# Gated attention plus token-mixing MLP: the last 24 attention visits in eight groups of three instead of twelve groups of two

## The chip, the cores and the metric

The kernel runs on one core of a Trainium2 chip. The metric is the device time of one execution in microseconds (us). Every time below comes from the runs of the kernel before or from the profile of one of its executions.

## The reference

The input x has S = 2048 tokens of D = 640 channels, in float32. Two branches read it and a gate mixes them:

```python
g = sigmoid((x * gate_w).sum(-1))
# attention: 32 heads of 20, one shared K and V
q = x @ wq; k = x @ wk; v = x @ wv
p = softmax(q k^T * 20**-0.5)          # per head, 2048 x 2048
a = concat_heads(p @ v) @ wo
# token mixing MLP
h = layernorm(x)
u = gelu(h^T @ w1 + b1)                # over tokens, F = 1728
b = (u @ w2 + b2)^T
out = g * a + (1 - g) * b
```

## The kernel before

**Units and visits.** Attention is cut into 32 units: four blocks of 512 queries times eight groups of four heads. For each unit the 2048 keys are walked in 16 blocks of 128, so there are 512 (unit, key block) pairs, which the code calls `units` and which I call visits. A visit needs four score tiles, one per head: `qk(u, pr, b)` issues one matmul of 62 rows by 512 columns on TensorE (L632) into a PSUM tile `s`, and one exponential on ScalarE (L635) from `s` into an SBUF tile `p`. The pool `ps_s` has three PSUM buffers, so the fourth score has to wait until the first exponential has read its tile, and so on; the pool `pp_pool` has twelve `p` buffers. `pv_mm(u)` then issues the four products with V (L659), which use four column tiles of 32 and accumulate over the unit's 16 visits in the one PSUM tile `o` (`ps_o`, one buffer). After a unit's last visit VectorE transposes `o` out of PSUM (L668), and the next unit's first product has to wait for that.

**Lanes.** A score needs 62 rows of the array only. Scores with b = 0 use rows 0 to 63 and those with b = 1 rows 64 to 127, and the other matmuls of the loop are cut into halves of 64 rows as well. The kernel writes out by hand (`manual_schedule`) an order in which the two row halves, the lanes, each have a list of work, and it interleaves the two lists by adding up estimated times: `X_US` = 0.232 us for a score, `F_US` = 0.147 us for a matmul with 320 columns. Each engine works through its instructions in the order in which they are written.

**The main loop.** For visits 0 to 487 each step k writes four scores in lane k % 2 (two of visit k - 1 and two of visit k) and other work in the other lane, then the four products of visit k - 1. Each head pair of a visit belongs to one lane, so half the scores of a visit are written one step early.

**The last 24 visits.** When the other work has run out (`TAIL` = 24, `k_tail` = 488), the lanes are filled with the output projection of the last eight blocks of 128 tokens. `tail_job(n)` (L773) puts its matmuls on the two lists `tail[0]` and `tail[1]`, 216 and 204 of them; `tail_take` takes the next ones from a list. They accumulate in the pools `ps_m` (three PSUM buffers) and `ps_g` (one), and each finished tile is scaled and added by VectorE (L780), which frees its buffer. `tail_load` fetches their operands by DMA (L754, L757). `stretch(k, n)` writes the scores of the steps k to k + n - 1 and their share of the tail matmuls, interleaved, and then the products of the visits k - 1 to k + n - 2, together. It is called once with n = 1 (the single) and then twelve times with n = 2 (the doubles). Where in a lane's list its scores stand is given by fixed fractions (`cut`) of its tail matmuls.

**Behind it.** After the last products come 24 matmuls of held partial sums (L1012), the chain that scales and splits the last unit's output (L668 to L685), 24 last matmuls (L1026) and the stores. `settle` pops pieces of the chain of an earlier unit, `visit` writes the products and, at two key blocks of a unit, the store and the fetch of the row maxima (L491, L498) that the next unit's scores need. These go on SyncE's DMA queue, as do the stores of finished output rows (L784).

Of the kernel before, what the change touches and what calls it, by code (L numbers as in the profile page):

```python
# [9 lines left out]
F32 = mybir.dt.float32  # L10
# [7 lines left out]
P = 128  # L18
# [6 lines left out]
NB = 512  # L25
# [12 lines left out]
def mix_kernel(ctx: ExitStack, tc: tile.TileContext, A_x, A_wq, A_wk, A_wv, A_wo,  # L38
               B_x, B_w1, B_b1, B_w2, B_b2, gate_w, out):
    nc = tc.nc  # L40
    x = A_x[0]
    y_out = out[0]

    def f32(ap):
        return ap.bitcast(F32)
# [30 lines left out]
    right = ExitStack()  # L76
# [73 lines left out]
    def new_q(n):  # L150
        if n < NU:
            qtiles[n] = load_q(n, "qst")
# [13 lines left out]
    with tc.tile_pool(name="pa", bufs=1) as pa, \  # L166
# [129 lines left out]
        def q_parts(m, ts):  # L296
            cols = slice(m * P, (m + 1) * P)
            return [[(wq_hi[:, c, cols], ts[c][0]) for c in range(DC)],
                    [(wq_hi[:, c, cols], ts[c][1]) for c in range(DC)],
                    [(wq_lo[:, c, cols], ts[c][0]) for c in (0, 3, 1, 4, 2)]]  # L300
# [88 lines left out]
        for sb in range(NQB):  # L389
# [11 lines left out]
            for m in range(DC):  # L401
# [3 lines left out]
                p = q_parts(m, ts)  # L405
# [36 lines left out]
    pp_pool = ctx.enter_context(tc.tile_pool(name="pp", bufs=12))  # L442
# [112 lines left out]
    with tc.tile_pool(name="psb", bufs=2, space=PSUM, side="right") as psb:  # L555
        at, skip, last = 0, 3, NS * PRO - 6
# [40 lines left out]
    oTs = [slot[1][:, 2 * DC * D + i * 2 * D:2 * DC * D + (i + 1) * 2 * D].rearrange("p (j c q) -> p j c q", j=2, q=P)  # L597
           for i in range(2)]
    yts = [f32(slot[1][:, 2 * DC * D + 4 * D + i * D:2 * DC * D + 4 * D + (i + 1) * D]) for i in range(2)]
    pools = {}  # L600

    def second():
        right.close()
        pools["rows"] = ctx.enter_context(tc.tile_pool(name="rows", bufs=3, side="right"))

    wos = {}
# [10 lines left out]
    units = [(n, kb) for n in range(NU) for kb in range(NS)]  # L617
# [4 lines left out]
    SYNC = mybir.DependencyInfo(mybir.DependencyClass.Sync, mybir.DependencyReason.DATA)  # L622
    odd_s = [0]

    def qk(u, pr, b):
        n, kb = units[u]
        if kb == 4 and pr == 0 and b == 0:
            new_q(n + 1)
        q = qtiles[n]
        odd_s[0] ^= 1  # L630
        s = ps_m.tile([P, NB], F32, name="ms") if spare[0] and odd_s[0] and not loaded else ps_s.tile([P, NB], F32, name="s")
        nc.tensor.matmul(s, kst[64 * b:64 * b + 62, kb * P:(kb + 1) * P], q[64 * b:64 * b + 62, pr, :],  # L632
                         start=True, stop=True)
        p = pp_pool.tile([P, NB], F32, name="p")
        nc.scalar.activation(p, s, AF.Exp, scale=SCALE)  # L635
        ptiles[u, 2 * pr + b] = p

# [97 lines left out]
    tail = [[], []]  # L735
    loaded = []
    CUT = 3 * P
    HEAD = (H - 4) * DH
    jobs = [(st, 0, D) for st in range(NS - 8, NS - 4)]
# [7 lines left out]
    def tail_load(i):  # L747
        if i < len(jobs):
            st, r0, r1 = jobs[i]
            cols = slice(st * P, (st + 1) * P)  # L750
            oT, yt = room(i)
            c0, c1 = r0 // P, r1 // P
            for j in range(2):
                nc.sync.dma_start(out=f32(oT[:, j, c0:c1]),  # L754
                                  in_=o_scr[j, r0:c1 * P, cols].rearrange("(c p) s -> p c s", p=P))
                if r1 > c1 * P:
                    nc.sync.dma_start(out=f32(oT[:r1 - c1 * P, j, c1]), in_=o_scr[j, c1 * P:r1, cols])  # L757
            if r0 == 0:
                nc.sync.dma_start(out=yt, in_=y_scr[cols, :])
            loaded.append(i)  # L760
# [31 lines left out]
    def tail_take(h, n):  # L792
        out = []
        while len(out) < n and tail[h] and tail[h][0][0] in loaded:
            out.append(tail[h].pop(0)[1])
        return out
# [56 lines left out]
    def b1_jobs(d, fc):  # L853
        hold = {}
        base = 4 * (d * FC + fc)

        def load():
            pass

        def mm(st, k, half):  # L860
            if not hold.get("n"):
                hold["p"], hold["n"] = ps_g.tile([P, NB], F32, name="g"), 0
            wh, wl = w1t[base + st // HS]
            w, h = ((wh, h_hi), (wh, h_lo), (wl, h_hi))[k]
            hold["n"] += 1
            r = slice(64 * half, 64 * half + 64)
            other_tile(half, nc.tensor.matmul(hold["p"][:, :HD2], w[r, st % HS, :], h[d][r, st, :],  # L867
                                              start=(hold["n"] == 1), stop=(hold["n"] == 6 * NS)))

        def done():  # L870
            gelu(d, fc, [hold["p"]])

        return load, [([[lambda h=h, st=st, k=k: mm(st, k, h) for h in range(2)]
                        for st in range(NS) for k in range(3)], done)]

    def batches(tiles, counts):
        out = []
        for n, (load, parts, *_) in enumerate(tiles):
            for d, (steps, done) in enumerate(parts):
                cnt = counts.pop(0)  # L880
                rows = [[f[h] for f in steps if len(f) > h] for h in range(2)]
                cut = [[len(r) * j // cnt for j in range(cnt + 1)] for r in rows]
                for j in range(cnt):
                    rest = []
                    if d == 0 and j == 0 and n + 1 < len(tiles):
                        rest.append(tiles[n + 1][0])
                    out.append(([r[c[j]:c[j + 1]] for r, c in zip(rows, cut)], rest, [done] if j == cnt - 1 else []))
        return out

    k_tail = len(units) - TAIL  # L890
    todo = [divmod(i, FC) for i in range(PRO, 2 * FC)]
    seq = batches([b1_jobs(*t) for t in todo], [5] * len(todo))
    for i, (steps, rest, done) in enumerate(seq):
        item, j = divmod(i + 1, 5)
# [17 lines left out]
    for i, k in enumerate((443, 451, 459, 467, 473, 477, 481, 485)):  # L912
        ph[k][1].append(lambda i=i: tail_load(i))

    X_US, F_US = 0.232, 0.147

    def beside(rows0, rows64, x):
        lanes = [list(rows0), list(rows64)]
        at = [0.0, 0.0]
        while lanes[0] or lanes[1]:  # L920
            k = 0 if lanes[0] and (not lanes[1] or at[0] <= at[1]) else 1
            if k == x and len(lanes[k]) == 1 and lanes[1 - k]:
                k = 1 - k
            us, f = lanes[k].pop(0)
            f()
            at[k] += us
# [15 lines left out]
    def settle(k):  # L942
        for _ in range(2 if spare[0] else 1):
            f = later.pop(0) if later else None
            if f:
                f()
        pop_chain()

    def visit(u):
        pv_mm(u)  # L950
        n, kb = units[u]
        if kb == 7 and n + 1 < NU:
            store_max(n + 1)
        if kb == 9 and n + 1 < NU:
            fetch_max(n + 1)

    for k in range(k_tail):
        b = k % 2
        ss = [lambda u=u, pr=pr: qk(u, pr, b) for u in (k - 1, k) for pr in range(2) if u >= 0]
        fs, rest, done = ph[k]  # L960
        ms = [[f for f in (ms_next(x) for _ in range(c)) if f] for x, c in (((b, 3), (1 - b, 1)) if len(fs) < 12 else ((b, 4), (1 - b, 0)))]
        lanes = [None, None]
        lanes[b] = lane_x(ss, ms[0])
        lanes[1 - b] = lane_f(ms[1], fs, done)
        if k == 0:
            (m0, m1, m2), (s0, s1) = ms[0], ss
            lanes[0] = [(3 * X_US, m0), (3 * X_US, m1), (X_US, s0), (X_US, m2), (X_US, s1)]
        beside(*lanes, b)
        ms_done()
        spare[0] = len(row_max) == NU  # L970
        settle(k)
        for f in rest:
            f()
        if k == k_tail - 4:
            raw = last_wo()
        if k == k_tail - 2:
            w_last = split_last(raw)
        if k:
            visit(k - 1)

    def stretch(k, n):
        lanes = [None, None]
        for b in range(2):
            own = [j for j in range(k, k + n) if j % 2 == b]
            ss = [lambda u=u, pr=pr, b=b: qk(u, pr, b) for j in own for u in (j - 1, j) for pr in range(2) if u < len(units)]
            fs = tail_take(b, math.ceil(len(tail[b]) * n / (len(units) + 1 - k)) + (n == 1) * (3 if not ss else -3))
            cut = [0] + [round(len(fs) * x) for x in ((0.25, 0.5, 0.75, 1.0) if n == 1 else
                                                          (0.18, 0.53, 0.82, 1.0) if b == k % 2 else (0.41, 0.71, 1.0, 1.0))]
            lanes[b] = [x for i in range(4) for x in [(X_US, y) for y in ss[i:i + 1]] +
                        [(F_US, f) for f in fs[cut[i]:cut[i + 1]]]]  # L990
        beside(*lanes, None)
        for j in range(k, k + n):
            settle(j)
            if 13 <= j - k_tail < 17:
                tail_load(8 + j - k_tail - 13)
            visit(j - 1)

    stretch(k_tail, 1)
    for k in range(k_tail + 1, len(units), 2):
        stretch(k, 2)  # L1000
    accs = {}

    for c in range(CUT // P, DC):
# [14 lines left out]
    for i in range(4):  # L1018
        st = NS - 4 + i
        for d in range(2):  # L1020
            at = pp_pool.tile([P, NB], F32, name="p")
# [34 lines left out]
```

## Time and profile before

| | |
|---|---|
| median of 3 runs (lowest to highest) | 1699.42 us (1699.42 to 1699.83) |
| the profiled execution's own time | 1699.95 us |
| its span, first to last instruction | 1698.2 us |
| visits 488 to 511, doubles only | 1617.84 to 1685.55 us of the span |
| behind the last products | 1685.55 to 1698.2 us |

How to read it: times are counted from the start of the span. A row of the timeline gives the start, the time from the start of the first to the end of the last of the instructions merged in the row, the engine, the line, the operation with its tiles, and the number of instructions. PE is TensorE (matmuls), PEld its weight loads, DVE VectorE, ACT ScalarE, POOL GpSimd, SPq the DMA issues of SyncE. Two row halves of the array work at once, so rows of PE overlap. A product with V stands as two instructions in the profile, hence x16 for two visits.

### The profile page before, as it was taken

Reading aid. Unit: us, or ns where it says so; the run is one execution under the profiler, and the core shown is the slowest. Engines: PE = TensorE matmul, PEld = TensorE weight load, DVE = VectorE, ACT = ScalarE, POOL = GpSimd, SP = SyncE. Lnnn points to the kernel's source line nnn. Section 1 sums busy time; section 2 is a strip of 40 time slices with the busy share of each in tenths; the row PEclk is TensorE's granted clock in tenths of the full one; section 3 lists DMA queues with packets and bytes.
Section 4 is the critical chain, followed back from the end, with each engine's and each line's share of the span. In section 5 each row is a group of like instructions: output and inputs, shape, how many; then the busy total and the mean of one; then the engine's idle time right before and its main releaser. Section 6 shows DMA issues by size and latency. Waiting matters only on the chain.

```text
span 1698.2 us, 39056 instructions
## 1 busy us (share of the span) xinstructions
PE 1690.9 (100%) x14865; PEld 1102.9 (65%) x14865; DVE 1434.7 (84%) x2915; ACT 1190.0 (70%) x2322; POOL 570.8 (34%) x723
## 2 busy tenths in 40 slices
PE   9999999999999999999999999999999999999998
PEld 7899766666666666666666666666666666555666
DVE  6679898888888888888888888888888888888734
ACT  4445677777777777777777777777777777777775
POOL 6467644544445454322222222222221111111200
PEclk9999999999999999999999999999999999999999
DMA  7665322222222222121212222222111222334411
GB/s 208 196 182 143 93 64 69 65 61 67 59 69 70 70 70 70 48 64 53 58 47 70 71 59 62 63 56 62 51 51 38 58 63 64 95 109 146 133 54 57
DMA packets 173377, 135.45 MB, mean 80 GB/s; under 512 B 32729, under 2 KB 139382, under 8 KB 173190
## 3 DMA queue, kind: packets, MB, share of 16 engines
q1 hardware_dynamic: 173190, 132.96, 28.0%
q8 instruction: 117, 1.92, 0.5%
q14 instruction: 70, 0.57, 0.1%
HBM read 100.27 MB, written 31.65 MB: 78 GB/s over the span
## 4 chain that ended last, share of the span: by engine, by line
PE 97%; issue 2%; DVE 1%; POOL 0%; ACT 0%; POOLq 0%; DVEq 0%; ACTq 0%
PE o L659 30%; PE s L632 18%; PE ms L466 17%; PE g L704 12%; PE g L867 8%; PE pp L293 4%; PE pu L576 4%; PE g L816 2%; PE ms L773 1%; PE pt L285 0%; PE pp L357 0%; DVE mp L469 0%; PE g L773 0%; PE pp L182 0%; PE pp L285 0%
## 5 line engine op out<-in xcount | busy, mean ns | idle before, releaser
L469 DVE TENSOR_REDUCE mp<-ms 128x1 f32<-128x512 f32 x2048 | 1278.6, 684 | 171.3 <-PE ms L466 167.2
L635 ACT ACTIVATE p<-s 128x512 f32<-128x512 f32 x2048 | 1069.1, 604 | 397.5 <-PE s L632 394.0
L466 PE MATMUL ms<-kst,qmx 60*128 60x512 f32 x2048 | 847.5, 421 | 0.7 <-DVE mp L469 0.5
L632 PE MATMUL s<-qst,kst 62*128 62x512 f32 x2048 | 745.6, 404 | 0.0
L659 PE MATMUL o<-p,v_sb 128*32 128x512 f32 x4096 | 554.6, 604 | 0.0
L466 PEld LDWEIGHTS ms<-kst,qmx 60*128 60x128 f32 x2048 | 378.0, 185 | 213.4 <-DVE flag L645 176.9
L632 PEld LDWEIGHTS s<-qst,kst 62*128 62x128 f32 x2048 | 378.0, 186 | 11.5 <-issue 10.9
L867 PE MATMUL g<-slot,wh 64*128 64x320 f32 x1152 | 281.6, 318 | 0.0
L124 POOL TENSOR_TENSOR wl<-wr,wh 128x512 fp32r<-128x512 f32 (+1 forms) x176 | 220.6, 1255 | 34.7 <-ACT wh L121 20.9
L867 PEld LDWEIGHTS g<-slot,wh 64*128 64x128 f32 x1152 | 190.6, 184 | 59.9 <-DVE flag L645 59.9
L123 POOL CAST wh<-wr 128x512 fp32r<-128x512 f32 (+1 forms) x136 | 79.7, 586 | 444.2 <-PE g L704 281.3
L704 PE MATMUL g<-slot,wh 64*128 64x320 f32 x864 | 209.0, 317 | 0.0
L704 PE MATMUL g<-u,wh 64*128 64x320 f32 x864 | 208.8, 317 | 0.0
L659 PEld LDWEIGHTS o<-p,v_sb 128*32 128x32 f32 x4096 | 93.3, 108 | 138.1 <-issue 130.8
L867 PE MATMUL g<-slot,wl 64*128 64x320 f32 x576 | 179.4, 311 | 0.0
L704 PEld LDWEIGHTS g<-slot,wh 64*128 64x128 f32 x864 | 142.3, 184 | 40.3 <-DVE flag L645 40.3
L704 PEld LDWEIGHTS g<-u,wh 64*128 64x128 f32 x864 | 142.3, 184 | 40.3 <-DVE flag L645 40.3
L704 PE MATMUL g<-u,wl 64*128 64x320 f32 x432 | 134.9, 313 | 0.0
L704 PE MATMUL g<-slot,wl 64*128 64x320 f32 x432 | 134.9, 313 | 0.0
L867 PEld LDWEIGHTS g<-slot,wl 64*128 64x128 f32 x576 | 106.0, 184 | 15.1 <-DVE flag L645 15.1
L704 PEld LDWEIGHTS g<-u,wl 64*128 64x128 f32 x432 | 79.5, 184 | 13.4 <-DVE flag L645 13.4
L704 PEld LDWEIGHTS g<-slot,wl 64*128 64x128 f32 x432 | 79.4, 184 | 13.4 <-DVE flag L645 13.4
(195 smaller groups left out, 1405.2 us busy)
## 6 DMA issues: line engine op xcount, KB each, us to landing
wr<-in_B_w_dram SPq DMA_DIRECT2D x152, 256.0 KB
qmx<-q_scr SPq DMA_DIRECT2D x192, 80.0 KB
qst<-q_scr SPq DMA_DIRECT2D x192, 80.0 KB
y_scr<-yo SPq DMA_DIRECT2D x16, 320.0 KB
slot<-o_scr SPq DMA_DIRECT2D x16, 320.0 KB
o_scr<-oh SPq DMA_DIRECT2D x124, 40.0 KB
o_scr<-ol SPq DMA_DIRECT2D x124, 40.0 KB
q_scr<-qh SPq DMA_DIRECT2D x19, 256.0 KB
```

What stands on the lines that cost most here:

```text
L123: nc.gpsimd.tensor_copy(wh, wr)
L124: nc.gpsimd.tensor_sub(wl, wr, f32(wh))
L293: nc.tensor.matmul(pp, w, t, start=first and n == 0, stop=not more and n == len(steps) - 1)
L466: nc.tensor.matmul(ms, qmax[n][64 * b:64 * b + 60, pr, qt * P:(qt + 1) * P], kst[64 * b:64 * b + 60, kq * NB:(kq + 1) * NB], start=True, s ...
L469: nc.vector.tensor_reduce(mtiles[n][:, c, kq:kq + 1], ms, axis=AX.X, op=ALU.max)
L576: nc.tensor.matmul(pu[r][:, :HD2], w[rows, c, :], h[rows, st, :], start=(st == 0 and k == 0), stop=(st == NS - 1 and k == 2))
L632: nc.tensor.matmul(s, kst[64 * b:64 * b + 62, kb * P:(kb + 1) * P], q[64 * b:64 * b + 62, pr, :], start=True, stop=True)
L635: nc.scalar.activation(p, s, AF.Exp, scale=SCALE)
L659: nc.tensor.matmul(o[32 * hh:32 * hh + 32, :], v_sb[:, kb, :], ptiles.pop((u, hh)), start=(kb == 0), stop=(kb == NS - 1), skip_group_check ...
L704: other_tile(half, nc.tensor.matmul(hold["p"][:, :HD2], w[r, fc % HS, :], u[d][r, fc, :], start=(hold["n"] == 1), stop=(hold["n"] == 6 * F ...
L816: other_tile(half, nc.tensor.matmul(hold["p"][:, :HD2], o[r, c, :], w[r, c, d * HD2:(d + 1) * HD2], start=(hold["n"] == 1), stop=(hold["n" ...
L867: other_tile(half, nc.tensor.matmul(hold["p"][:, :HD2], w[r, st % HS, :], h[d][r, st, :], start=(hold["n"] == 1), stop=(hold["n"] == 6 * NS)))
```

## The change

`stretch` is called once with n = 1 and then eight times with n = 3 (the triples). It no longer places the scores by fixed fractions. It makes one sequence of all scores of the group, sorted by visit, and gives number i (from 0) the target time (i - 2) x `EXP_US`, with `EXP_US` = 0.45. Each lane then takes its next score as soon as the lane's added-up time has reached that target, and a tail matmul otherwise. The share of the tail matmuls that a lane gets is worked out so that both lanes are about equally long, since in a triple one lane has eight scores and the other four. Two more SBUF tiles for `p` are allocated (`extra_p`) where buffers of the finished weight stream were, and `next_p` uses them as numbers 1 and 2 of a cycle of 14.

```diff
+        xp = ctx.enter_context(tc.tile_pool(name="xp", bufs=1, side="right"))
+        extra_p.extend(xp.tile([P, NB], F32, name=f"p{i}") for i in range(2))
...
+    turn_p = [0]
+
+    def next_p():
+        turn_p[0] += len(loaded) >= len(jobs) - 4
+        i = turn_p[0] % 14
+        return extra_p[i - 1] if 0 < i < 3 else pp_pool.tile([P, NB], F32, name="p")
...
-        p = pp_pool.tile([P, NB], F32, name="p")
+        p = next_p()
...
-    X_US, F_US = 0.232, 0.147
+    X_US, F_US, EXP_US = 0.232, 0.147, 0.45
...
     def stretch(k, n):
-        lanes = [None, None]
-        for b in range(2):
-            own = [j for j in range(k, k + n) if j % 2 == b]
-            ss = [lambda u=u, pr=pr, b=b: qk(u, pr, b) for j in own for u in (j - 1, j) for pr in range(2) if u < len(units)]
-            fs = tail_take(b, math.ceil(len(tail[b]) * n / (len(units) + 1 - k)) + (n == 1) * (3 if not ss else -3))
-            cut = [0] + [round(len(fs) * x) for x in ((0.25, 0.5, 0.75, 1.0) if n == 1 else
-                                                          (0.18, 0.53, 0.82, 1.0) if b == k % 2 else (0.41, 0.71, 1.0, 1.0))]
-            lanes[b] = [x for i in range(4) for x in [(X_US, y) for y in ss[i:i + 1]] +
-                        [(F_US, f) for f in fs[cut[i]:cut[i + 1]]]]
-        beside(*lanes, None)
+        ss = [[], []]
+        seq = []
+        for j in range(k, k + n):
+            b = j % 2
+            new = [(b, u, pr) for u in (j - 1, j) for pr in range(2) if u < len(units)]
+            seq += new
+        seq.sort(key=lambda x: (x[1], x[0] != k % 2))
+        for i, (b, u, pr) in enumerate(seq):
+            ss[b].append((max(0.0, (i - 2) * EXP_US), lambda u=u, pr=pr, b=b: qk(u, pr, b)))
+        left = len(units) + 1 - k
+        own = [sum(2 * X_US for j in range(k, len(units) + 1) if j % 2 == b for u in (j - 1, j) if u < len(units))
+               for b in range(2)]
+        fs = [tail_take(b, len(tail[b]) if n == left else
+                        max(0, round(((own[b] + len(tail[b]) * F_US) * n / left - len(ss[b]) * X_US) / F_US)))
+              for b in range(2)]
+        at = [0.0, 0.0]
+        while any(ss) or any(fs):
+            b = 0 if at[0] <= at[1] and (ss[0] or fs[0]) or not (ss[1] or fs[1]) else 1
+            if ss[b] and (ss[b][0][0] <= at[b] or not fs[b]):
+                ss[b].pop(0)[1]()
+                at[b] += X_US
+            else:
+                fs[b].pop(0)()
+                at[b] += F_US
         for j in range(k, k + n):
             settle(j)
...
-    for k in range(k_tail + 1, len(units), 2):
-        stretch(k, 2)
+    for k in range(k_tail + 1, len(units), 3):
+        stretch(k, 3)
```

More of the change, by code (lines that the diff above doesn't have):

```diff
@@ L599, in mix_kernel @@
     yts = [f32(slot[1][:, 2 * DC * D + 4 * D + i * D:2 * DC * D + 4 * D + (i + 1) * D]) for i in range(2)]
-    pools = {}
+    pools, extra_p = {}, []
     def second():
         right.close()
+        xp = ctx.enter_context(tc.tile_pool(name="xp", bufs=1, side="right"))
+        extra_p.extend(xp.tile([P, NB], F32, name=f"p{i}") for i in range(2))
         pools["rows"] = ctx.enter_context(tc.tile_pool(name="rows", bufs=3, side="right"))
```

## The prediction

> **What bounds the kernel now.** I read the page first, then the busy time of the engines in the stretch of the last 24 visits, then the timeline of TensorE, ScalarE and VectorE inside it, row by row.
>
> ```profile
> span 1698.2 us, 39056 instructions
> ...
> PE 97%; issue 2%; DVE 1%; POOL 0%; ACT 0%; POOLq 0%; DVEq 0%; ACTq 0%
> ...
> L635 ACT ACTIVATE p<-s 128x512 f32<-128x512 f32 x2048 | 1069.1, 604 | 397.5 <-PE s L632 394.0
> ```
>
> ```profile
> 1617.84:1685.55 67.71, 67.71 (x693) 45.89 (x689) 23.10 (x44) 47.50 (x94) 1.91 (x2) 1.00 0.12 37
> ```
>
> The columns of the second fence are the window, its length, then busy time of PE, weight loads, VectorE, ScalarE and GpSimd, the granted clock and the DMA share. The chain of waits is TensorE nearly all through, and in the twelve doubles (67.71 us) it is never idle, at full clock. ScalarE has 47.5 us of work there, all of it exponentials: a third of its time is free on average. What counts is when in a double they run.
>
> ```profile
> 1633.10 1.92 PE L659 MATMUL o<-p,v_sb 128*32 128x512 f32 x16
> 1634.95 0.50 PE L632 MATMUL s<-qst,kst 62*128 62x512 f32 x2
> 1635.29 0.31 PE L773 MATMUL ms<-slot,u 64*128 64x320 f32 x1
> ...
> 1635.44 0.31 PE L773 MATMUL ms<-slot,u 64*128 64x320 f32 x1
> ...
> 1635.58 0.31 PE L773 MATMUL ms<-slot,u 64*128 64x320 f32 x1
> ...
> 1635.73 0.39 PE L632 MATMUL s<-qst,kst 62*128 62x512 f32 x1
> ...
> 1636.32 0.39 PE L632 MATMUL s<-qst,kst 62*128 62x512 f32 x1
> ...
> 1636.70 0.42 PE L632 MATMUL s<-qst,kst 62*128 62x512 f32 x1
> ...
> 1637.43 0.39 PE L632 MATMUL s<-qst,kst 62*128 62x512 f32 x1
> ...
> 1637.69 0.41 PE L632 MATMUL s<-qst,kst 62*128 62x512 f32 x1
> ...
> 1638.45 0.40 PE L632 MATMUL s<-qst,kst 62*128 62x512 f32 x1
> ```
>
> ```profile
> 1629.82 4.03 ACT L635 ACTIVATE p<-s 128x512 f32<-128x512 f32 x8 [1.64 <-PE s L632]
> 1635.49 4.03 ACT L635 ACTIVATE p<-s 128x512 f32<-128x512 f32 x8 [1.64 <-PE s L632]
> ```
>
> One double: products at 1633.10, eight scores from 1634.95 to 1638.45 with tail matmuls between them. The first exponential starts 0.54 us after the first score, the eight run back to back in 4.03 us, then ScalarE idles 1.64 us until the next group. One exponential takes 0.60 us (604 ns on the page), so they follow each other every (4.03 - 0.60) / 7 = 0.49 us. With three score buffers, score i (from 0) needs the end of exponential i - 3. That of exponential 2 is at 1635.49 + 2 x 0.49 + 0.60 = 1637.07, of exponential 1 at 1636.58: score 4 starts at 1636.70, 0.12 behind it, and score 6 at 1637.69, 0.13 behind the end of exponential 3. I take 0.12 as the time from an exponential's end to the score; it is an upper bound, since these scores stand about there in their lane anyway. So the doubles already feed ScalarE as fast as it empties the buffers, with the pauses between groups left over.
>
> **The change part by part.**
>
> *Fewer changes between lanes and products.*
>
> ```profile
> 1614.80 0.49 PE L632 MATMUL s<-qst,kst 62*128 62x512 f32 x1
> ...
> 1616.84 1.06 PE L659 MATMUL o<-p,v_sb 128*32 128x512 f32 x8
> 1617.84 0.50 PE L632 MATMUL s<-qst,kst 62*128 62x512 f32 x2
> ...
> 1668.54 0.50 PE L632 MATMUL s<-qst,kst 62*128 62x512 f32 x2
> ...
> 1672.21 1.92 PE L659 MATMUL o<-p,v_sb 128*32 128x512 f32 x16
> ...
> 1679.59 0.50 PE L632 MATMUL s<-qst,kst 62*128 62x512 f32 x2
> ...
> 1683.69 1.92 PE L659 MATMUL o<-p,v_sb 128*32 128x512 f32 x16
> 1685.55 1.58 PE L1012 MATMUL ms<-slot,slot 128*128 128x320 f32 x9
> ```
>
> Products of one visit hold TensorE 1.00 us (1616.84 to 1617.84), of two 1.86 (1683.69 to 1685.55): 0.86 a visit and 0.14 fixed; of three 2.72. The lane part of a double is 3.67 us (1668.54 to 1672.21) where its longer list holds four scores and 17 matmuls, 4 x 0.232 + 17 x 0.147 = 3.43: 0.24 fixed. Four groups fewer save 4 x (0.14 + 0.24) = 1.5 us. The Trainium skill speaks for this edit: "TensorEngine Tiling (Array Packing)", Key Properties, says that a change of tiling mode drains the engine. The fixed 0.38 us of a group agrees with it.
>
> *The target times.* Run through with the constants of the program, the list of a triple has twelve scores and 50 tail matmuls and is 5.2 us long in its longer lane; its first four scores come after 0, 2, 4 and 5 of the tail matmuls or so, the fourth (i = 3) at 0.70 in list time, the twelfth (i = 11) at 4.1. Against that stands what ScalarE allows. Score i can start 0.54 + (i - 3) x 0.49 + 0.60 + 0.12 = 1.26 + 0.49 (i - 3) after the first: 1.26 for the fourth, 5.18 for the twelfth. The targets (i - 2) x 0.45 leave out the 0.54 and most of the 0.60 + 0.12 that stand ahead of the first release, and their step is 0.04 under the pace. TensorE takes its queue in order: behind a waiting score stand the tail matmuls of both lanes, and behind those the products. So the fourth score stops both lanes for about half a microsecond, and the following ones keep them at ScalarE's pace until the twelfth at 5.18. Between two scores stand three to six tail matmuls, 0.2 to 0.45 us in each of two lanes, less than 0.49, so nothing is made up. After the twelfth the list has 5.2 - 4.1 = 1.1 us left, and from the lanes' end to the products are 0.1 us (score at 1638.45, 0.232 long, next products 1638.77). The lane part of a triple is 5.18 + 1.1 + 0.1 = 6.4 us, less 0.05 for the scores that stand in the lighter lane: 6.35. Bounds: with a release of 0 in place of 0.12, 6.23; with a pace of 0.48, 8 x 0.01 less.
>
> The Trainium skill, "ScalarE: Activation LUTs", What ACT_TABLE_LOAD costs, gives an activation 186 ns + 0.833 ns an element and an overlap of 93 ns back to back: for 512 columns 0.61 us, as the rows, but a step of 0.52. By it a triple is 8 x 0.03 = 0.24 us longer, the whole 1.9 us. The measured 0.49 decides.
>
> *Eight triples.* 6.35 + 2.72 = 9.07 us each, 72.6 in all.
>
> *The last triple* has ten scores and 54 tail matmuls. Its tenth score starts at 1.26 + 6 x 0.49 = 4.20; 24 tail matmuls follow, 12 a lane, 1.76, with half a score and the end 0.2: 6.2. Many short accumulations end there, and the four PSUM buffers come free only after VectorE. The last double of before shows such waits: 1679.59 to 1683.69 is 4.10 where its list of 3.28 + 0.24 gives 3.52: 0.58. Here a longer row of tail matmuls stands together; I take 0.8 (between 0.58 and twice that), so 7.0, which is 0.65 over a plain triple.
>
> *A unit's end inside a triple.* Visits 495 and 496 are of two units. Before, they are in different doubles; now the third triple holds 494, 495, 496, and the products of 496 stand in TensorE's queue right behind those of 495, while `o` has one buffer.
>
> ```profile
> 1640.63 0.50 PE L632 MATMUL s<-qst,kst 62*128 62x512 f32 x2
> ```
>
> ```profile
> 1640.79 0.72 DVE L668 STREAM_TRANSPOSE ot<-o 128x512 f32<-128x512 f32 x1 [1.38 <-PE o L659]
> ```
>
> Where the next work of TensorE would start (1640.63), the transpose has not begun; it ends at 1641.51. With 0.1 for the release (as the scores' 0.12) the stall is 1.0 us, bare, since nothing but products and the next group stands behind it. Before it lies under the lanes.
>
> *The single* loses its fixed fractions too: fourth score at 1.26 in place of list time 0.70, then the list's remaining 1.66 - 0.70 and 0.1: 2.32, against 2.04 (1614.80 to 1616.84): +0.28.
>
> *Edits at nothing.* Twelve exponentials of a triple and two kept from the one before fill 14 `p` buffers, freed by the products ahead: no wait. With twelve, the last two exponentials would wait for the first products. The stores and fetches on SyncE's queue keep their order but for one swap: the fetch of the last unit's row maxima now stands behind the store of the first finished tail row.
>
> ```profile
> 1617.89 2.74 SPq L498 DMA_DIRECT2D qst<-m_scr  x4
> 1625.64 19.24 SPq L784 DMA_DIRECT2D out_dram<-yo  x3
> ```
>
> So it is issued at about 1627 in place of 1617.9, 2.74 us for four. Its first reader is the end of the third triple's scores, about 1641. Cover: over 10 us; without it each us late would be a us lost. VectorE's order changes by a few places among rows of 0.55 us, under 23.1 us of work in 67.7.
>
> *Sum.* 72.6 + 0.65 + 1.0 + 0.28 - 67.71 = +6.8 us; rounded down for the pace of 0.48 that a part of the exponentials may have, +6.6. The profiled execution's own time is 1699.95 (span 1698.2 and 1.75 around it), so 1706.55; the median of the runs is 0.5 lower, so 1706.1.
>
> **The rivals.**
>
> *The scores don't hold the lanes* (the opposite side: not slower). Mechanism: the release comes early enough at the fourth score, so that a triple takes list time. It decides from a release before 0.70 us after the first score. Then a triple is 5.2 + 0.24 + 2.72 = 8.16, eight 65.3; with 1.0 for the transpose, 0.65 for the last and -0.14 for the single 66.8, against 67.71: -0.9 us, 1698.5 by the median. This is what the drain rule of the skill would bring, less the transpose. For it: the target times are made for just this, ScalarE idles 1.64 us a group. Against: the first exponential cannot end before 0.54 + 0.60 = 1.14, and no row shows one faster.
>
> *The end piles up.* The last triple's bank waits and the late rows cost more: 24 tail matmuls with some five changes of buffer, each up to 1 us (0.55 for VectorE's row, the rest for the matmul's end and the releases), are up to 3 us over the 0.8 taken, and held matmuls behind would wait too: 1708 to 1709. For it: the 0.58 in a shorter row. Against: most of these evictions overlap other matmuls.
>
> *Half the loss:* with release 0 and pace 0.48, 8 x (0.12 + 0.08) = 1.6 less, and a shorter transpose wait: 1704.3. It is the low end of my own case.
>
> **How the numbers follow.** About 0.2% (3.4 us) is what a measurement here can tell from no change. My case, 0.80, from 1704.3 to 1707.8; the pile-up 0.10, to 1709; the held list 0.10, around 1698.5, of which a fifth falls beyond 0.2% faster if the transpose and the last triple cost nothing too. Slower by over 0.2% 0.90, within 0.08, faster 0.02. The range 1703.0 to 1708.8 covers my case with its bounds and nearly all of the pile-up.
>
> **What would show it.** In the profile after: eight groups of about 9.0 us in the last 24 visits; the fourth score some 1.2 us behind the first and each following one about 0.48 behind; twelve exponentials back to back in about 5.9 us; TensorE's 1.0 us pause inside the third triple with the transpose in it; the products of three visits in 2.72. Wrong would be: scores at the list's times, or groups under 8.5 us.

## The result and the profile after

| | before | after |
|---|---|---|
| median of the runs, us | 1699.62 (4 runs, 1699.42 to 1699.83) | 1706.86 (4 runs, 1706.81 to 1707.77) |
| ratio to before | | 1.0044, interval 1.0031 to 1.0056 |
| profiled execution: own time, span | 1699.95, 1698.2 | 1707.77, 1706.0 |

The kernel became 7.2 us slower; 1706.1 was forecast, with a range of 1703.0 to 1708.8. The profiled execution after is the highest of its four runs. Its span is 7.8 us longer: 7.0 us in the groups behind the single, 0.36 in the single, and 0.44 ahead of it, since the single starts at 1615.24 where it started at 1614.80. That last part isn't the change's: in the profiles of the experiments below, where the code up to there is that of after, the single starts between 1614.06 and 1615.20.

The busy time of the engines, for the eight triples and for what follows them (the columns as in the prediction's second fence):

```profile
1618.63:1693.37 74.74, 71.47 (x695) 48.63 (x691) 23.82 (x44) 46.90 (x94) 1.88 (x2) 1.00 0.11 33
1693.37:1706.00 12.63, 7.79 (x52) 7.08 (x48) 5.64 (x10) 2.13 (x4) 2.56 (x3) 1.00 0.29 104
```

74.74 us stand where 67.71 stood, and the part behind the products is as long as before (12.63 against 12.65). ScalarE's work is the same (46.9 against 47.5 us of busy time). TensorE counts as busy in 71.47 of 74.74 us. So 3.3 of the 7.0 us that are lost there show as idle time, and the share hides the rest: PE counts as busy where only one of the two row halves works, and where a row is drawn to the start of the next one. The waits of TensorE's matmuls over the same stretch, with the single (engine and line, what it waited for: total us, times, longest):

```profile
PE s L641 <- ACT p L644: 2.3, 9, 0.3
PE o L668 <- DVE ot L677: 0.8, 1, 0.8
PE g L782 <- DVE row L789: 0.4, 1, 0.4
```

Nine waits of a score for an exponential: one in the single and one in each triple. The weight loads of TensorE (PEld), which are listed apart, wait more often for the same thing, twice in each triple:

```profile
PEld s L641 <- ACT p L644: 6.2, 17, 0.5
```

Before, neither matmuls nor weight loads of scores wait for an exponential in this stretch. What such a wait does is to be read in the timeline of a triple, the third, TensorE's scores and products, with the ends of the last triple and one tail matmul of it below them:

```profile
1636.92 0.50 PE L641 MATMUL s<-qst,kst 62*128 62x512 f32 x1
1637.26 0.40 PE L641 MATMUL s<-qst,kst 62*128 62x512 f32 x1
1637.49 0.40 PE L641 MATMUL s<-qst,kst 62*128 62x512 f32 x1
1638.16 0.50 PE L641 MATMUL s<-qst,kst 62*128 62x512 f32 x1 [0.26 <-ACT p L644]
1638.65 0.50 PE L641 MATMUL s<-qst,kst 62*128 62x512 f32 x1
1639.14 0.50 PE L641 MATMUL s<-qst,kst 62*128 62x512 f32 x1
...
1641.66 0.42 PE L641 MATMUL s<-qst,kst 62*128 62x512 f32 x1
1642.08 0.49 PE L641 MATMUL s<-qst,kst 62*128 62x512 f32 x1
1643.29 1.92 PE L668 MATMUL o<-p,v_sb 128*32 128x512 f32 x16
1646.05 1.06 PE L668 MATMUL o<-p,v_sb 128*32 128x512 f32 x8 [0.84 <-DVE ot L677]
1647.05 0.49 PE L641 MATMUL s<-qst,kst 62*128 62x512 f32 x1
...
1683.60 0.50 PE L641 MATMUL s<-qst,kst 62*128 62x512 f32 x1
...
1687.79 0.49 PE L641 MATMUL s<-qst,kst 62*128 62x512 f32 x1
...
1689.41 0.41 PE L782 MATMUL g<-slot,slot 64*128 64x320 f32 x1 [0.41 <-DVE row L789]
...
1690.65 2.78 PE L668 MATMUL o<-p,v_sb 128*32 128x512 f32 x24
1693.36 0.86 PE L1035 MATMUL ms<-slot,slot 128*128 128x320 f32 x4
```

and ScalarE and VectorE around it:

```profile
1628.32 5.99 ACT L644 ACTIVATE p<-s 128x512 f32<-128x512 f32 x12 [3.10 <-PE g L782]
1637.51 5.99 ACT L644 ACTIVATE p<-s 128x512 f32<-128x512 f32 x12 [3.20 <-PE ms L782]
```

```profile
1645.28 0.72 DVE L677 STREAM_TRANSPOSE ot<-o 128x512 f32<-128x512 f32 x1 [2.30 <-PE o L668]
```

The fourth score starts 1.24 us after the first, the next ones 0.49 apart (1638.16, 1638.65, 1639.14), the twelfth 5.16 after the first; after it the lanes run on for 1.21 us until the products. The first exponential starts 0.59 us after the first score, ends 0.60 later, and the fourth score starts 0.05 behind that end; TensorE as a whole stands idle for 0.26 us ahead of it. The exponentials run back to back, twelve in 5.99 us, then ScalarE idles 3.2 us. A waiting score stands as 0.50 long in place of 0.39, as the first score of each group does, behind the products. At the end of the second visit's products the transpose of `o` starts at 1645.28, and the third visit's products start at 1646.05, 2.76 us after the first pair; in the other triples the products of three visits are one row.

### The profile page after: what moved, and what is told of

Its sections match the earlier page's. It is cut to its first block, busy times and chain, and to the rows that moved or that the text cites. A ratio compares the mean times of both kernels' runs of the same rounds, so it can differ in the third digit from the quotient of the medians.

```text
span 1706.0 us, 39052 instructions
## 1 busy us (share of the span) xinstructions
PE 1695.0 (99%) x14865; PEld 1105.7 (65%) x14865; DVE 1435.1 (84%) x2915; ACT 1188.8 (70%) x2322; POOL 570.6 (33%) x723
## 4 chain that ended last, share of the span: by engine, by line
PE 95%; issue 2%; DVE 1%; SPq 1%; DMA 0%; ACT 0%; POOL 0%; POOLq 0%; DVEq 0%; ACTq 0%
PE o L668 30%; PE s L641 18%; PE ms L466 17%; PE g L713 12%; PE g L876 8%; PE pp L293 4%; PE pu L576 4%; PE g L825 2%; PE ms L782 1%; DMA xa<-in_A_x_dram 0%; DVE mp L469 0%; PE pt L285 0%; PE g L782 0%; ACT p L644 0%; SPq L190 0%
```

## The experiments

Two theories were set against each other. The first is the prediction's: with three score buffers ScalarE's release sets when the scores can start, the target times stand ahead of it, and a waiting score holds both lanes. The second: the grouping in threes is what costs (24 products in a row, a unit's end inside a group, a crowded end). Each run below starts from the kernel after; times of before are those of the same chip (1699.5 to 1699.8 us on the chips used).

**Corrected targets in triples.**

```diff
-    X_US, F_US, EXP_US = 0.232, 0.147, 0.45
+    X_US, F_US, EXP_US = 0.232, 0.147, 0.49
-            ss[b].append((max(0.0, (i - 2) * EXP_US), lambda ...
+            ss[b].append((0.0 if i < 3 else 1.26 + (i - 3) * EXP_US, lambda ...
```

> Triples as in the change, but the targets follow what ScalarE allows: scores 0 to 2 at once, score i from 3 on at 1.26 + 0.49 (i - 3). If the score buffers' release sets the length of a triple (my theory), no score waits any more, a triple falls from 9.1 to 8.2 to 8.4 us, and the total to 1699.5 us (1698.8 to 1701). If the loss lies in the grouping itself (24 products in a row, the unit's end inside a triple, the crowded end), the total stays above 1705.

Measured 1701.19 us (11 runs) against 1699.83 for before: ratio 1.0008, interval 0.9999 to 1.0017. 5.7 us of the loss are gone, with nothing moved but the scores among the tail matmuls; the total is a little above the upper end of what was expected. TensorE's scores in its third triple:

```profile
1633.73 0.50 PE L641 MATMUL s<-qst,kst 62*128 62x512 f32 x1
...
1635.12 0.39 PE L641 MATMUL s<-qst,kst 62*128 62x512 f32 x1
1635.59 0.40 PE L641 MATMUL s<-qst,kst 62*128 62x512 f32 x1
...
1638.41 0.49 PE L641 MATMUL s<-qst,kst 62*128 62x512 f32 x1
1638.89 0.50 PE L641 MATMUL s<-qst,kst 62*128 62x512 f32 x1
1639.53 1.92 PE L668 MATMUL o<-p,v_sb 128*32 128x512 f32 x16
```

The fourth score stands at 1.39 us and no longer waits; the twelfth still starts 5.16 after the first. In the list it stands at 4.7, ahead of its target, because its lane has run out of tail matmuls; its weight load waits:

```profile
1638.89 0.18 PEld L641 LDWEIGHTS s<-qst,kst 62*128 62x128 f32 x1 [0.30 <-ACT p L644]
```

So ScalarE's pace holds there, and against the expectation one score or two still wait in each triple but the last. What is left behind the twelfth is 0.64 us in place of 1.21. The lane part is 5.80 us, or 5.6 in the triples whose list ends with its scores; the list with its fixed part would be 5.2 + 0.24. So even rightly timed triples are bound by the twelfth score.

**The offset alone, and the step alone.** One run keeps the step of 0.45 and corrects the offset (the second line of the diff above), one corrects the step to 0.49 and keeps (i - 2).

> Triples with the offset corrected and the step left: scores 0 to 2 at once, score i at 1.26 + 0.45 (i - 3). My theory: the missing offset is most of the loss. The twelfth score still starts at 5.17 and stands at 4.86 in the list, so some 0.4 us of list are behind it: a lane part of 5.7 to 5.8 us, total 1701.5 us (1700.8 to 1702.5). If the step were the main fault, over 1703.5.

> Triples with the step corrected and the offset left: score i at (i - 2) x 0.49. My theory: the fourth score still stops both lanes at 0.8 until 1.25 us; the twelfth stands at 4.41 in the list and has 0.8 us behind it: a lane part of 6.1 to 6.2 us, total 1704.9 us (1704 to 1705.7). If the step is the main fault, 1702 or less.

Offset alone: 1700.86 us (10 runs; ratio 1.0008, interval 0.9999 to 1.0017). Step alone: 1704.76 us (6 runs; 1.003, 1.0019 to 1.0041). The offset is worth 6.0 us, the step 2.1, both together 5.7: with the offset right, the step of 0.45 does no harm.

**The change's targets in doubles.**

```diff
-    for k in range(k_tail + 1, len(units), 3):
-        stretch(k, 3)
+    for k in range(k_tail + 1, len(units), 2):
+        stretch(k, 2)
```

> The change's target times (i - 2) x 0.45, but in doubles. My theory: in each double the eighth score can start at 1.26 + 4 x 0.49 = 3.2 us and has 1.1 us of list behind it, so the lane part is 4.4 us where it was 3.7; twelve of them, without the transpose stall of 1 us: 1708 us (1706.5 to 1710), slower than the triples. If the grouping in threes is what costs: 1699.6 as before.

1710.34 us (4 runs), ratio 1.0062, interval 1.0048 to 1.0075: slower than the triples, and above what was expected by 0.3 us: the lane parts are 4.50 to 4.66 us where 4.4 was reckoned, and 5.42 in the last double. In doubles the loss of each group is paid twelve times. One of them:

```profile
1637.01 0.50 PE L641 MATMUL s<-qst,kst 62*128 62x512 f32 x1
...
1638.25 0.49 PE L641 MATMUL s<-qst,kst 62*128 62x512 f32 x1 [0.25 <-ACT p L644]
...
1640.23 0.48 PE L641 MATMUL s<-qst,kst 62*128 62x512 f32 x1
1641.52 1.92 PE L668 MATMUL o<-p,v_sb 128*32 128x512 f32 x16
```

The fourth score at 1.24, the eighth at 3.22, the products at 4.51 where a double of before had them at 3.67 to 3.87 (4.10 in the last). The second theory, which expects 1699.6 here, falls.

**Shorter exponentials.** In the last 24 visits only 256 of 512 columns go through the exponential; GpSimd sets the rest of `p` to 1.

```diff
-        nc.scalar.activation(p, s, AF.Exp, scale=SCALE)
+        if u >= k_tail:
+            nc.gpsimd.memset(p[:, NB // 2:], 1.0)
+            nc.scalar.activation(p[:, :NB // 2], s[:, :NB // 2], AF.Exp, scale=SCALE)
+        else:
+            nc.scalar.activation(p, s, AF.Exp, scale=SCALE)
```

> The change with the exponentials of the last 24 visits cut to 256 of the 512 columns (the other half of p is set to 1 by GpSimd, so that part of the attention is left out). An exponential takes about 0.39 us and the pace is about 0.28, so the fourth score is released at 1.05 us in place of 1.26 and all later ones are ahead of the list. My theory: a triple of 8.4 us, total 1701 us (1700 to 1703). If TensorE's own order or the grouping sets the triples: above 1705.

1702.04 us (8 runs), ratio 1.0013, interval 1.0003 to 1.0023: 4.8 us of the loss gone with TensorE's order untouched and half of the exponentials of these visits left out. The third triple in its trace, TensorE's first, fourth and twelfth score and the products:

```profile
1635.51 0.49 PE L641 MATMUL s<-qst,kst 62*128 62x512 f32 x1
...
1636.56 0.49 PE L641 MATMUL s<-qst,kst 62*128 62x512 f32 x1
...
1640.09 0.39 PE L641 MATMUL s<-qst,kst 62*128 62x512 f32 x1
1641.21 1.07 PE L672 MATMUL o<-p,v_sb 128*32 128x512 f32 x8
```

The fourth score starts 1.05 us after the first, as reckoned, the twelfth at 4.58, the products at 5.70 where they were at 6.37.

**A group that ends with the unit.** Groups of 3, 3, 2, 3, 3, 3, 3, 2, 2 visits, first with the change's targets, then with the corrected ones.

```diff
-    for k in range(k_tail + 1, len(units), 3):
-        stretch(k, 3)
+    k = k_tail + 1
+    for n in (3, 3, 2, 3, 3, 3, 3, 2, 2):
+        stretch(k, n)
+        k += n
```

> The change's target times with groups of 3, 3, 2, 3, 3, 3, 3, 2, 2 visits, so that the unit ends with a group. My theory: the stall of 1.05 us behind the transpose goes; three doubles with the list's loss cost 0.2 us more each than their share of triples: 1706.3 us (1705.6 to 1707). If the stall of the third triple were made up elsewhere, no less than 1707.

> Corrected targets with groups of 3, 3, 2, 3, 3, 3, 3, 2, 2: no unit ends inside a group. My theory: against the triples with corrected targets the stall of 1.05 us goes, and one more group comes in with 0.4 us of fixed cost: 0.6 us under them, 1700.3 us (1699.6 to 1701), and not under the doubles with corrected targets (1698.6), since the twelfth score of a triple cannot start before 5.17 us while the lists end at 5.2. If triples are the better grouping once timed rightly, 1698.4 or less.

With the change's targets 1706.93 us (4 runs; ratio 1.0042, 1.0028 to 1.0056): the same as after, where 0.6 us less was expected. The pause behind the transpose is gone from its trace, and the doubles give the time back: one of them, in TensorE's scores and products:

```profile
1636.08 0.50 PE L641 MATMUL s<-qst,kst 62*128 62x512 f32 x1
...
1640.58 1.92 PE L668 MATMUL o<-p,v_sb 128*32 128x512 f32 x16
1642.44 0.49 PE L641 MATMUL s<-qst,kst 62*128 62x512 f32 x1
```

It takes 6.36 us, where two thirds of a triple's 9.1 are 6.07. With the corrected targets 1699.28 us (11 runs; ratio 0.9999, 0.999 to 1.0008), 1.9 us under the plain triples (1.6 when each is taken against before on its own chip). That is 1.0 us better than I expected, and the reason is in my reckoning: I charged one more group with 0.4 us of fixed cost, but a double with corrected targets has no wait and costs 3.64 + 1.85 us for two visits, 8.24 for three, while a triple costs 5.6 to 5.8 + 2.71. So putting doubles in the place of triples is itself a gain.

**Without the two extra buffers** for `p` (`next_p` always takes from the pool of twelve).

> The change without its two extra p buffers. My reckoning: the last two exponentials of a triple wait for the products of its first visit (some 1 us after the products start) and are done before the next triple's first score needs their score buffers, so nothing is lost: 1706.9 us (1706.4 to 1707.4). If twelve buffers hold up the group, each triple loses about 0.5 us or more: 1710 and above.

1706.91 us (4 runs), ratio 1.0043, interval 1.0029 to 1.0057: as after. ScalarE's rows in one of its triples:

```profile
1637.02 5.01 ACT L643 ACTIVATE p<-s 128x512 f32<-128x512 f32 x10 [1.08 <-PE ms L781]
1643.96 1.08 ACT L643 ACTIVATE p<-s 128x512 f32<-128x512 f32 x2 [1.93 <-PE o L667]
1647.10 5.01 ACT L643 ACTIVATE p<-s 128x512 f32<-128x512 f32 x10 [2.06 <-PE s L640]
```

The last two exponentials do wait for the products (L667), and end 2 us before the next ten begin. The wait is there and costs nothing.

**Corrected targets in doubles:** the two edits of the first run and the loop of the fourth.

> Doubles again, with the corrected targets (0 for scores 0 to 2, then 1.26 + 0.49 (i - 3)) and the change's sharing of the tail matmuls between the lanes. My theory: the eighth score stands at 3.2 us, as ScalarE allows, and nearly ends the list, so no score waits; the lanes' lists are 3.43 us where the first six doubles of before had 3.57, there is no transpose in a group, and the single is 0.2 us shorter: 0.5 to 1 us under before, 1698.7 to 1699.4 us. If the sorted list with targets costs something of its own, over 1700.5.

1698.62 us (11 runs, 1698.36 to 1698.99) against 1699.71 for before (23 runs, 1699.31 to 1700.72): ratio 0.9993, interval 0.9984 to 1.0002. That is 0.1 us under what was expected. No run of the one lies within the runs of the other, though the interval just holds 1. In the profiles the stage, from the single to the end of the last products, takes 69.71 us (1614.86 to 1684.57) against 70.75 before (1614.80 to 1685.55). One of its doubles:

```profile
1634.17 0.49 PE L641 MATMUL s<-qst,kst 62*128 62x512 f32 x1
...
1635.54 0.39 PE L641 MATMUL s<-qst,kst 62*128 62x512 f32 x1
...
1637.46 0.41 PE L641 MATMUL s<-qst,kst 62*128 62x512 f32 x1
1637.80 1.92 PE L668 MATMUL o<-p,v_sb 128*32 128x512 f32 x16
```

The eighth score at 3.29 us, where ScalarE lets it start at 3.22, and the products 0.34 behind it: release and list end together, and the lane part is 3.63 us. It is the fastest version of this case, about 1 us under before and 8 us under after.

## Why the prediction was right

*Fourth score stopped at 1.26 us, then ScalarE's pace:* right. Measured 1.24, then 0.49 a score, the twelfth at 5.16 (5.18 forecast). That the first is so close is in part luck: the first exponential starts 0.59 us after the first score where 0.54 was taken, and the release takes 0.05 where 0.12 was, so two errors nearly cancel. Run alone, the offset is the greater part of the loss (6.0 us), as the prediction's split of the lateness has it: 0.56 at the fourth score at once, 0.04 at each following one.

*A waiting score holds both lanes:* right. Ahead of the fourth score TensorE as a whole is idle, so neither lane works. The scores alone were moved in the first experiment, and 5.7 us came back. That the release is ScalarE's doing and not an order of TensorE's own is shown by the shorter exponentials.

*The lane part of a triple, 6.35 us:* a little short. It is 6.37 in the third triple (1636.92 to 1643.29) and some 0.1 more in every second one, of which 0.05 is in the lists (5.19 and 5.24 us in the longer lane); the rest stays open. The 0.05 that I took off for the scores in the lighter lane, and the lower pace of 0.48 for which I rounded the sum from 6.8 to 6.6, are not in the rows: twelve exponentials in 5.99 us are (5.99 - 0.60) / 11 = 0.49 each. Seven triples by some 0.07, with the single (2.40 measured, 1615.24 to 1617.64, against 2.32), are the 0.5 us by which the stage's 7.4 exceeds my sum of 6.8.

*Products of three visits 2.72:* right (2.71). The saving of fewer groups, which was priced at 1.5 us with them, could not show as long as the lanes waited. With corrected targets it does not show either: the triples there are slower than the doubles, since the lane part of a triple ends behind the twelfth score at 5.16. Of the fixed 0.38 us of a group, the 0.14 beside the products are borne out; what the 0.24 in the lane part consist of, no run separates.

*The transpose stall, 1.0 us:* right; from the first products to the next matmul behind them are 3.76 us in the third triple (1643.29 to 1647.05) and 2.71 in the last (1690.65 to 1693.36): 1.05. Its removal gained nothing by itself in the run with other groups, since each double under the change's targets costs 0.3 us more than its share of a triple.

*The last triple, 0.65 over a plain one:* right in size: 7.05 us of lane part (1683.60 to 1690.65) where I had 7.0. That it is 2.86 us from the tenth score to the products, for 24 tail matmuls that would fill 1.76, fits the bank waits. The trace names one of them, 0.41 us at 1689.41, where a matmul into `g` waits for VectorE; no run takes them away, so that the rest is their doing too is only argued.

*Edits at nothing:* right. The trace shows no wait for a `p` buffer, and without the two buffers the time is the same. The fetch of the row maxima was issued at 1626.21, as forecast, and no score waits for it.

*The rival of the held list* needed a release before 0.70 us. It came at 1.24, and at 1.05 even with half the exponential left out. The corrected targets, which take the wait of the fourth score away, come to 1701, not 1698.5: their triples take 8.3 to 8.5 us where the rival had 8.16, and the twelfth score still waits there. *The pile-up* did not come: the last triple's lane part is 0.85 over its 6.2 without bank waits, where 0.8 was taken.

## What to carry to other kernels

When a list places work that needs buffers from another engine, its target times need the whole way to the first release (start, duration, signal; 1.24 us here), and not only the pace; correcting a step 8% under the pace gained 2 us by itself, and nothing once the offset was right; correcting the offset gained 6. A larger group must also be checked against the slowest resource inside it: three buffers and 0.49 us a score put the twelfth score at 5.16 us, which eats what the saved group changes (reckoned at 0.38 us each) bring. And the busy share of a TensorE that two row halves share hid over half of the loss: read the distances between the matmuls, and the waits of the weight loads too.

## What was not expected of the hardware

The waits that the profile names on TensorE's matmuls add up to 2.3 us for the scores, where 7 us were lost: only the first wait of each triple has a gap of its own. On the weight loads of the scores it names 6.2 us. The rest of the loss shows as scores that stand as 0.49 to 0.50 us long in place of 0.39, 0.49 apart, and as list time left over behind the last score. And the start of the last stage moves by up to 1.2 us from one profiled execution to another with the same work ahead of it (1614.06 to 1615.24 in the profiles here), which is more than the gain of the best version; that gain could be read only within the stage, and over many runs.
